# Closing the first two tiles of expert 0 one pair of batches earlier, in an attention and mixture-of-experts kernel

## The chip, the core and the metric

The kernel runs on one core of a Trainium2 chip. The core has TensorE (PE) for matrix products, VectorE (DVE), ScalarE (ACT) and GpSimd (POOL) for the rest, and SyncE (SP), which here only issues transfers; ACT and POOL issue some too. Each engine works through its own instructions in order and waits for others by semaphores. What is measured is the device time of one execution in microseconds (us); lower is better.

## The reference

A sliding-window attention (8 batches, 8 heads, 576 tokens, head size 64, window 64) gives a matrix x of 4608 tokens by 512. A mixture of 8 experts then takes each token to the one expert with the largest logit, with no token dropped:

```python
scores = scale * np.matmul(q, k.transpose(0, 1, 3, 2))
mask = (rel >= 0) & (rel < window)            # window = 64
...
x = attn_out.transpose(0, 2, 1, 3).reshape(B * S, H * D)
logits = x @ w_gate
expert_idx = np.argmax(logits, axis=1)
gate_w = probs[np.arange(N), expert_idx]
...
for e in range(E):
    h = np.maximum(x_sorted[lo:hi] @ w1[e], 0.0)   # 512 -> 1024
    y_sorted[lo:hi] = h @ w2[e]                    # 1024 -> 512
...
return (gate_w[:, None] * y)
```

All of it is in float32.

## The kernel before

**Attention.** Batches are taken in four pairs (`bg` 0 to 3, 1152 tokens each, held as 9 groups of 128), and each pair in four pairs of heads. A pair of batches and a pair of heads is a unit; there are 16 units of 3 steps, so N = 48 steps. `step(s)` (line 896) writes out by hand, in one order for all engines, pieces of several steps at once: scores of step s+1 (`scored`, line 550, into PSUM banks 0 and 1), mask and maximum (`masked`, DVE line 585), exponentials (ACT line 595), the product with v of step s-1 (`weighted`, line 618, bank 6), the logits of step s-3 (line 655, bank 7), transposes of the probabilities of step s (`flipped`, lines 603 and 605), the division (`divided`, DVE lines 628 to 632), transposes of q and k for step s+3 (lines 539 and 531) and of x for step s-2 (`x_turned`, line 643). Then come the operations that were put down in `todo` for this step.

**Routing.** When a pair's logits are there, `after` (line 833) spreads over the next steps: `choose` (line 677) in five parts, which finds the expert, the gate and each token's rank within its expert, and adds to `count`; `place` (line 744), two DVE operations (line 746) for each group of 128 tokens, which write one-hot rows of token numbers; `weigh` (line 751), which multiplies the 512 values of 128 tokens by their gates; and `store` (line 759), which writes the scaled x to `x_dram`. The last pair's routing is written out after the loop, between the products of the first tile.

**Tiles.** The experts work on tiles of 256 tokens, gathered from `x_dram` by indirect transfers that POOL issues. The list of tokens in each slot, `perm_i`, is itself made by products of one-hot tables (`slot_table`, line 779; PE line 807, 72 products). Tiles 0 and 1, both of expert 0, don't wait for that list: `first_tiles` (line 857) picks their 512 tokens out of the first three pairs with a smaller table of its own, `hi_e`, and 54 products (line 869) into `perm_e`. So that no later token gets a slot in them, `choose` sets the count of expert 0 to at least 512 after the third pair (line 730). `gather_first` (line 277) gathers the rows into `xg`.

One tile is a chain of generators: `hidden` (line 314), seven products (PE line 322) in a Strassen form, whose sums of w1 are made ahead on POOL; `turn` (line 299), eight transposes of the next tile's rows (PE line 303) copied by ACT (line 304) to `xq`; and `output` (line 367), seven products (PE line 362), with `sums_x` (DVE line 311), four sums of the turned rows, and four DVE sums of the hidden values (line 139). `sums_w2` (line 152) makes the four sums of w2 on POOL (line 139), into the memory of q and k turned. After the attention loop (line 932 on) the pieces of tile 0 and of the last pair's routing alternate by hand: `next(tile0)` issues one product of the tile, `next(routing)` one part of `choose`, `weigh_some` three scalings on ACT and their store on SP. Tile 0's rows are gathered in step 45 by `first_tiles`, tile 1's after the loop. Two lines set the order around the change:

```python
for n, s in enumerate((N - 6, N - 3)):    # halves of w2 of expert 0, on SP
for _ in range(8):                        # line 984: next(tile0); next(table, None)
```

Behind tile 1 the loop over the experts follows (line 1000 on), with its bodies under conditions on the counts, and at the end `finish` and a last `scatter` (line 288), two indirect transfers to the output, which are declared as having no dependence on the other scatters.

Of the kernel before, what the change touches and what calls it, by code (L numbers as in the profile page):

```python
# [36 lines left out]
def kernel(  # L37
# [10 lines left out]
    nc = tc.nc  # L48
# [164 lines left out]
    hi_e = rt.tile([P, NJE, NE * C], BF16, name="hi_e")  # L213
# [63 lines left out]
    def gather_first(tokens):  # L277

        for c in range(C):
            G.memset(xg[c], 0.0)  # L280

            G.indirect_dma_start(
                out=xg[c], out_offset=None, in_=x_dram[0 : NT - BG * S, :],
                in_offset=bass.IndirectOffsetOnAxis(ap=tokens[:, c : c + 1], axis=0),
                bounds_check=NT - BG * S - 1, oob_is_err=False,
            )
# [12 lines left out]
    def turn():  # L299

        for c in range(C):
            for g in range(NG):
                nc.tensor.transpose(out=tps[c][:, g, :], in_=xg[c][:, g * P : (g + 1) * P], identity=ident[:])  # L303
            nc.scalar.copy(out=xq[:, :, c], in_=tps[c].rearrange("p (a g) s -> p a g s", a=2))
        yield

    def sums_x():
# [132 lines left out]
    with tc.manual_schedule(), ExitStack() as held, ExitStack() as brief:  # L440
# [236 lines left out]
        def choose(bg):  # L677
# [50 lines left out]
            if bg == last - 1:  # L728

                V.tensor_scalar_max(count[:, 0:1], count[:, 0:1], float(NE * TB))  # L730
# [48 lines left out]
        def slot_table(hi):  # L779
# [29 lines left out]
            for j in range(NJE):  # L809
                fill(j)  # L810
            for n in range(NST):
                for m in range(ST):
                    place(NJE + n * ST + m)
                yield
# [18 lines left out]
        def after(s, routing, bg):  # L833
# [3 lines left out]
            if bg < last - 1:  # L837
# [8 lines left out]
                return  # L846

            for n in (0, 0, 1, 2, 2):
                do(n, part)
            for m in range(NTB):  # L850
                do(3 + m // 3, partial(place, bg * NTB + m))
                do((2, 2, 3, 3, 4, 4, 4, 5, 5)[m], partial(weigh, bg, m, nc.scalar if m in (2, 6) else G))
                if m % ST == ST - 1:
                    do(3 + m // ST, partial(store, bg, m // ST, G))
            do(6, first_tiles)

        def first_tiles():

            V.scalar_tensor_tensor(
                out=key[:], in0=rkhi[:, 0:NJE], scalar=1.0, in1=oh_all[:, 0, 0:NJE], op0=ALU.add, op1=ALU.mult  # L860
            )
            V.tensor_tensor(
                out=hi_e[:], in0=_inner(key[:], NE * C), in1=_ins(hi_id[:, C + 1 : C + 1 + NE * C], 1, NJE),
                op=ALU.is_equal,
            )
            slots = banks[next(tr_ring)](0, NE * C)
            for j in range(NJE):
                for i in range(2):
                    nc.tensor.matmul(
                        slots, lhsT=lo[:, i, j], rhs=hi_e[:, j], start=(i + j == 0), stop=(i + j == NJE)  # L870
                    )
            V.tensor_scalar(out=perm_e[:], in0=slots, scalar1=-1.0, scalar2=float(NT), op0=ALU.mult, op1=ALU.add)
            gather_first(perm_e[:, 0:C])
# [55 lines left out]
        for n, s in enumerate((N - 6, N - 3)):  # L929
            fs = slice(n * HF, (n + 1) * HF)  # L930
            todo.setdefault(s, []).append(partial(nc.sync.dma_start, out=w2s[0][:, fs], in_=w2v[0][:, fs]))
        for s in range(-3, N):
            step(s)
        assert not todo
        sums_w2(0)
# [4 lines left out]
        tile0 = chain(hidden(0), turn(), output(0))  # L940
        px = weighted(N - 1, pTs.pop(N - 1))
        form_all(turn())
# [3 lines left out]
        sums_x()  # L946
        gather_first(perm_e[:, C : 2 * C])
        by_tok = [by_tokens(last, c) for c in range(NST)]
        next(by_tok[0])
        next(tile0)  # L950
        logit(N - 2)
        x_turned(N - 1)
        next(by_tok[0], None)
# [23 lines left out]
        next(tile0)  # L977
        next(routing, None)
        weigh_some(2)
# [4 lines left out]
        for _ in range(8):  # L984
            next(tile0)
            next(table, None)
        assert next(tile0, None) is None
# [55 lines left out]


# [26 lines left out]
```

## Time and profile before

| | |
|---|---|
| timed runs, median of 3 | 765.55 us (763.72 to 765.71) |
| the profiled execution, own time | 764.28 us |
| its span, first to last instruction | 762.4 us |
| busy: PE / DVE / ACT / POOL | 94% / 52% / 35% / 47% |
| granted PE clock, mean | 0.986 |
| step 39 of the attention starts | 169.65 us |
| last attention product (line 618) ends | 213.9 us |
| turn of tile 1's rows (line 303) starts | 230.05 us |
| products of the full slot table end | about 247.3 us |
| last scatter starts | 758.05 us |

Busy time is the time in which an engine has an instruction under way; a busy PE isn't PE at its peak, since products are pipelined. The clock is the share of full speed that PE was granted. In a timeline a row is a group of like instructions: start, duration, engine, line, operation, what is written and read, and in brackets how long the engine stood idle before it and which instruction ended that. Line numbers are those of the kernel before.

### The profile page before, as it was taken

What the parts mean: (1) busy time and instruction counts of PE and PEld (TensorE: products, weight loads), DVE (VectorE), ACT (ScalarE), POOL (GpSimd) and SP (SyncE); (2) the same over time, 40 slices, a digit from 0 to 9 for tenths busy, and PEclk for the clock granted to TensorE, in tenths of its full rate; (3) what the DMA queues carried; (4) which work ended last, traced back from release to release, by engine and by line L of the source; (5) the groups of instructions that cost most, each with busy time, mean ns of one, the idle gap of its engine ahead of it and who ended that gap; (6) DMA issues with size and microseconds to landing.
All of it is one profiled execution on the core that took longest, in us unless ns stands there. A gap on an engine that the chain in (4) does not pass through costs nothing. (4 is left out here: it accounts for less than half of the span.)

```text
span 762.4 us, 18401 instructions
## 1 busy us (share of the span) xinstructions
PE 720.1 (94%) x7018; PEld 650.5 (85%) x7018; DVE 395.0 (52%) x1355; ACT 268.4 (35%) x676; POOL 357.1 (47%) x366
## 2 busy tenths in 40 slices
PE   4999999999899999999999999999999999999995
PEld 3888888887688988998999899899988899988994
DVE  2677997988758544523542353352434452424432
ACT  4888888887543201211121122011220121211220
POOL 5215558593860635537531653663266465262111
PEclk8999999999899999999999999999999999999998
DMA  8997889983513712604410360542171171101101
GB/s 162 226 205 173 175 181 255 213 225 113 195 42 126 277 58 67 229 29 138 159 56 30 96 208 30 166 142 70 31 257 45 40 254 56 43 24 42 43 29 54
DMA packets 137620, 94.55 MB, mean 124 GB/s; under 512 B 117072, under 2 KB 117072, under 8 KB 137490
## 3 DMA queue, kind: packets, MB, share of 16 engines
q1 hardware_dynamic: 127858, 62.16, 29.8%
q0 software_dynamic: 9056, 28.58, 11.7%
q10 hardware_dynamic: 576, 2.10, 0.8%
q8 instruction: 78, 1.28, 0.7%
q14 instruction: 52, 0.43, 0.2%
HBM read 73.94 MB, written 20.45 MB: 124 GB/s over the span
## 5 line engine op out<-in xcount | busy, mean ns | idle before, releaser
L322 PE MATMUL bank<-qk_m,s 128*128 128x128 f32 x1216 | 145.4, 275 | 0.0
L322 PEld LDWEIGHTS bank<-qk_m,s 128*128 128x128 f32 x1216 | 140.4, 192 | 0.0
L322 PE MATMUL bank<-qk_m,w 128*128 128x128 f32 x912 | 112.2, 276 | 12.5 <-DVE v_m L358 8.8
L272 POOL DMA_INDIRECT qk_m<-x_dram,at_g x42 | 44.6, 1063 | 167.5 <-PE bank L303 160.2
L322 PEld LDWEIGHTS bank<-qk_m,w 128*128 128x128 f32 x912 | 106.7, 192 | 17.5 <-issue 17.3
L595 ACT ACTIVATE pr<-pr,mx 128x128 f32<-128x128 f32 x288 | 89.7, 390 | 31.8 <-DVE mx L585 31.5
L358 DVE TENSOR_TENSOR v_m<-bank,v_m 128x256 f32<-128x256 f32 x101 | 40.8, 422 | 110.1 <-PE bank L362 54.8
L585 DVE CUSTOM_DVE_ANT_0 pr<-bank,mask 128x128 f32<-128x128 f32 x288 | 64.4, 286 | 27.7 <-PE bank L572 26.1
L329 ACT COPY qk_m<-bank 128x512 f32<-128x512 f32 x19 | 11.2, 587 | 165.7 <-PE bank L322 155.2
L292 POOL DMA_INDIRECT out_dram<-v_m,at_s x42 | 42.4, 1010 | 56.5 <-DVE v_m L358 44.7
L139 POOL TENSOR_TENSOR s<-w 128x1024 f32<-128x1024 f32 x22 | 52.3, 2376 | 19.1 <-DMA qk_m<-x_dram,at_g 14.8
L362 PE MATMUL bank<-qkT_m,v_m 128*128 128x256 f32 x240 | 54.0, 380 | 1.7 <-DVE v_m L139 1.7
L362 PEld LDWEIGHTS bank<-qkT_m,v_m 128*128 128x128 f32 x240 | 45.4, 190 | 8.5 <-DVE v_m L139 2.5
L362 PE MATMUL bank<-qk_m 128*128 128x256 f32 x224 | 52.1, 380 | 0.0
L513 POOL COPY v_m<-v_m 64x520 f32<-64x520 f32 x32 | 19.8, 618 | 67.0 <-DMA v_m<-in_v_dram 59.7
L618 PEld LDWEIGHTS bank<-v_m,pT 128*64 128x64 f32 x1152 | 40.5, 139 | 11.6 <-DVE xs L632 5.8
L618 PE MATMUL bank<-v_m,pT 128*64 128x65 f32 x1152 | 47.2, 229 | 2.6 <-DVE xs L632 2.6
L362 PE MATMUL bank<-s,v_m 128*128 128x256 f32 x216 | 48.1, 379 | 0.0
L362 PEld LDWEIGHTS bank<-qk_m 128*128 128x128 f32 x224 | 41.5, 190 | 5.5 <-ACT v_m L374 0.4
L362 PEld LDWEIGHTS bank<-s,v_m 128*128 128x128 f32 x216 | 41.0, 190 | 5.6
L572 PE MATMUL bank<-qkT_m 64*64 64x128 f32 x1152 | 44.8, 286 | 0.1
L539 PE MATMUL bank<-ident,qk_m 128*128 128x128 f32 x256 | 36.6, 287 | 8.7 <-DMA qk_m<-in_q_dram 8.1
(167 smaller groups left out, 1220.7 us busy)
## 6 DMA issues: line engine op xcount, KB each, us to landing
w<-in_moe_w_dram SPq DMA_DIRECT2D x11, 2048.0 KB, 9.2
qk_m<-in_q_dram SPq DMA_DIRECT2D x72, 128.0 KB, 3.8
qk_m<-in_k_dram SPq DMA_DIRECT2D x72, 128.0 KB, 3.7
v_m<-in_v_dram SPq DMA_DIRECT2D x64, 128.0 KB, 3.7
qk_m<-in_moe_w_dram SPq DMA_DIRECT2D x3, 2048.0 KB, 16.1
x_dram<-xs POOLq DMA_DIRECT2D x6, 512.0 KB, 4.8
x_dram<-xs POOLq DMA_DIRECT2D x3, 768.0 KB, 5.3
w<-in_moe_w_dram ACTq DMA_DIRECT2D x4, 512.0 KB, 5.0
```

Source lines behind the costliest of these rows:

```text
L139: op()
L272: G.indirect_dma_start(out=xg[c], out_offset=None, in_=x_dram[:, :], in_offset=bass.IndirectOffsetOnAxis(ap=at_g[:, c : c + 1], axis=0),)
L292: put = G.indirect_dma_start(out=out[:, :], out_offset=bass.IndirectOffsetOnAxis(ap=at_s[:, c : c + 1], axis=0), in_=ys[c], in_offset=None ...
L322: nc.tensor.matmul(acc[:, f, :], lhsT=a[:, g, f * P : (f + 1) * P], rhs=b[:, g, :], start=(first and f == 0 and g == 0), stop=(g == HG - 1 ...
L358: plus = lambda out, a, b: V.tensor_tensor(out=out, in0=a, in1=b, op=ALU.add)
L362: nc.tensor.matmul(acc, lhsT=a[:, f, :], rhs=b[:, f, :], start=(start and f == 0), stop=(stop and f == HF - 1), skip_group_check=True,)
L513: nc.gpsimd.tensor_copy(out=vb[0:D, i].rearrange("p j h d -> p (j h d)"), in_=va[D:P, i].rearrange("p j h d -> p (j h d)"),)
L539: nc.tensor.transpose(out=tr.rearrange("d a b -> d (a b)").rearrange("d (p j) -> d j p", j=NV)[:, j, :], in_=t[:, c, j].rearrange("p h d - ...
L572: nc.tensor.matmul(out_, lhsT=qT[rows, t, a * WINDOW : (a + 1) * WINDOW], rhs=rhs, start=True, stop=True, skip_group_check=True,)
L585: V.tensor_tensor_reduce(out=prs[h][:, m, :], in0=scs[h][:, m, :], in1=mask[:, m0 + m, :], scale=-scale, scalar=-2 * MASKED, op0=ALU.add, ...
L595: nc.scalar.activation(out=y, in_=y, func=AF.Exp, scale=-1.0, bias=mx[:, h, m : m + 1])
L618: nc.tensor.matmul(px[a * D : (a + 1) * D, h, m, :], lhsT=pTs[h][:, m, a * D : (a + 1) * D], rhs=vt[:, h, :], start=True, stop=True, skip_ ...
```

## The change

Tile 0 is filled from the first two pairs alone (`count` of expert 0 is set to at least 256 after the second pair, and to at least 512 after the third), and tile 1 from the first three, so each gets its own small table: `first_tile(n)` replaces `first_tiles` and is a generator with two halves, the table on DVE and then the products, the list and the gather. Tile 0's halves go to steps N-10 and N-9; its turn and `sums_x` to step N-2, with banks 0 and 1 for the turned rows, and its first hidden product to step N-1. `sums_w2(0)` moves from behind the loop to step N-1, and the halves of w2 are loaded one step earlier. The halves of tile 1's table stand in the tail around the second hidden product.

For the third pair, the five parts of `choose` go to five steps, not three; its scalings are all on POOL, its stores on SP, and its `place` operations two to three steps later. In the tail the last three scalings on ACT move behind the turn of tile 1, and in `slot_table` the 54 products of the early groups move behind the second trio of `place`. At the very end POOL writes one column of each output buffer `ys`, which it can do only when the last scatter has read them.

```diff
@@ -210,7 +210,7 @@
     early, at, rk = (rt.tile([P, NJ], F32, name=n) for n in ("early", "at", "rk"))
     NJE = NJ - NTB
     key = rt.tile([P, NJE], BF16, name="key")
-    hi_e = rt.tile([P, NJE, NE * C], BF16, name="hi_e")
+    hi_e = rt.tile([P, NJE, C], BF16, name="hi_e")
     at_b = rt.tile([P, NJ], BF16, name="at_b")
 
     def starts():
@@ -274,15 +274,15 @@
                 in_offset=bass.IndirectOffsetOnAxis(ap=at_g[:, c : c + 1], axis=0),
             )
 
-    def gather_first(tokens):
+    def gather_first(tokens, rows):
 
         for c in range(C):
             G.memset(xg[c], 0.0)
 
             G.indirect_dma_start(
-                out=xg[c], out_offset=None, in_=x_dram[0 : NT - BG * S, :],
+                out=xg[c], out_offset=None, in_=x_dram[0:rows, :],
                 in_offset=bass.IndirectOffsetOnAxis(ap=tokens[:, c : c + 1], axis=0),
-                bounds_check=NT - BG * S - 1, oob_is_err=False,
+                bounds_check=rows - 1, oob_is_err=False,
             )
 
     def scatter(tokens):
@@ -296,7 +296,7 @@
             tc.declare_no_dep(put.ins, group="puts", reason="every token has one slot, so no row is written twice")
             tc.add_to_no_dep_group("puts", put.ins)
 
-    def turn():
+    def turn(tps=tps):
 
         for c in range(C):
             for g in range(NG):
@@ -304,7 +304,7 @@
             nc.scalar.copy(out=xq[:, :, c], in_=tps[c].rearrange("p (a g) s -> p a g s", a=2))
         yield
 
-    def sums_x():
+    def sums_x(tps=tps):
 
         b12, b22, b21 = tps[1][:, 0:HG], tps[1][:, HG:], tps[0][:, HG:]
         for n, (a, b) in enumerate(((b12, xq[:, 0, 0]), (b22, xs[:, 0]), (b22, xq[:, 0, 1]), (xs[:, 1], b21))):
@@ -725,9 +725,9 @@
             rank = new("r_rank", E, NTB)
             V.tensor_tensor(out=rank[:], in0=inc[:], in1=_inner(count[:], NTB), op=ALU.add)
             V.tensor_tensor(out=count[:], in0=count[:], in1=inc[:, :, NTB - 1], op=ALU.add)
-            if bg == last - 1:
-
-                V.tensor_scalar_max(count[:, 0:1], count[:, 0:1], float(NE * TB))
+            if last - NE <= bg < last:
+
+                V.tensor_scalar_max(count[:, 0:1], count[:, 0:1], float((bg - last + NE + 1) * TB))
             V.tensor_tensor(out=rank[:], in0=rank[:], in1=ranks[:, 1], op=ALU.subtract)
             V.tensor_tensor(out=rank[:], in0=rank[:], in1=ranks[:, 0], op=ALU.add)
             yield
@@ -806,11 +806,12 @@
                 for i in range(2):
                     nc.tensor.matmul(slots, lhsT=lo[:, i, j], rhs=hi[:, j], start=(i + j == 0), stop=(i + j == NJ))
 
-            for j in range(NJE):
-                fill(j)
             for n in range(NST):
                 for m in range(ST):
                     place(NJE + n * ST + m)
+                if n == 1:
+                    for j in range(NJE):
+                        fill(j)
                 yield
             for j in range(NJE, NJ):
                 fill(j)
@@ -844,33 +845,36 @@
                     if m % ST == ST - 1:
                         do(5 + m * 2 // 3, partial(store, bg, m // ST, G))
                 return
-
-            for n in (0, 0, 1, 2, 2):
+            for n in range(5):
                 do(n, part)
+
             for m in range(NTB):
-                do(3 + m // 3, partial(place, bg * NTB + m))
-                do((2, 2, 3, 3, 4, 4, 4, 5, 5)[m], partial(weigh, bg, m, nc.scalar if m in (2, 6) else G))
+                do((5, 5, 6, 6, 7, 7, 8, 8, 8)[m], partial(place, bg * NTB + m))
+                do((3, 3, 4, 4, 5, 5, 6, 6, 7)[m], partial(weigh, bg, m, G))
                 if m % ST == ST - 1:
-                    do(3 + m // ST, partial(store, bg, m // ST, G))
-            do(6, first_tiles)
-
-        def first_tiles():
-
+                    do(5 + m // ST, partial(store, bg, m // ST, nc.sync))
+
+        def first_tile(n):
+
+            nj = (last - NE + n + 1) * NTB
             V.scalar_tensor_tensor(
-                out=key[:], in0=rkhi[:, 0:NJE], scalar=1.0, in1=oh_all[:, 0, 0:NJE], op0=ALU.add, op1=ALU.mult
+                out=key[:, 0:nj], in0=rkhi[:, 0:nj], scalar=1.0, in1=oh_all[:, 0, 0:nj], op0=ALU.add, op1=ALU.mult
             )
             V.tensor_tensor(
-                out=hi_e[:], in0=_inner(key[:], NE * C), in1=_ins(hi_id[:, C + 1 : C + 1 + NE * C], 1, NJE),
-                op=ALU.is_equal,
-            )
-            slots = banks[next(tr_ring)](0, NE * C)
-            for j in range(NJE):
+                out=hi_e[:, 0:nj], in0=_inner(key[:, 0:nj], C),
+                in1=_ins(hi_id[:, (n + 1) * C + 1 : (n + 2) * C + 1], 1, nj), op=ALU.is_equal,
+            )
+            yield
+            slots = banks[next(tr_ring)](0, C)
+            for j in range(nj):
                 for i in range(2):
                     nc.tensor.matmul(
-                        slots, lhsT=lo[:, i, j], rhs=hi_e[:, j], start=(i + j == 0), stop=(i + j == NJE)
+                        slots, lhsT=lo[:, i, j], rhs=hi_e[:, j], start=(i + j == 0), stop=(i + j == nj)
                     )
-            V.tensor_scalar(out=perm_e[:], in0=slots, scalar1=-1.0, scalar2=float(NT), op0=ALU.mult, op1=ALU.add)
-            gather_first(perm_e[:, 0:C])
+            to = perm_e[:, n * C : (n + 1) * C]
+            V.tensor_scalar(out=to, in0=slots, scalar1=-1.0, scalar2=float(NT), op0=ALU.mult, op1=ALU.add)
+            gather_first(to, nj * P)
+            yield
 
         N = NU * NST
         load_qk(0)
@@ -926,30 +930,36 @@
                     after(s + 1, choose(bg), bg)
 
 
-        for n, s in enumerate((N - 6, N - 3)):
+        for n, s in enumerate((N - 7, N - 4)):
             fs = slice(n * HF, (n + 1) * HF)
             todo.setdefault(s, []).append(partial(nc.sync.dma_start, out=w2s[0][:, fs], in_=w2v[0][:, fs]))
+
+        tile0 = chain(hidden(0), turn(), output(0))
+        first = first_tile(0)
+        todo.setdefault(N - 10, []).append(partial(next, first))
+        todo.setdefault(N - 9, []).append(partial(next, first))
+        free = [banks[i](0, NG, P) for i in (0, 1)]
+        todo.setdefault(N - 2, []).extend((lambda: form_all(turn(free)), partial(sums_x, free)))
+        todo.setdefault(N - 1, []).extend((partial(next, tile0), partial(sums_w2, 0)))
         for s in range(-3, N):
             step(s)
         assert not todo
-        sums_w2(0)
 
 
 
         tr_ring = cycle((4, 5))
-        tile0 = chain(hidden(0), turn(), output(0))
         px = weighted(N - 1, pTs.pop(N - 1))
-        form_all(turn())
         logit(N - 3)
         divided(N - 1, px)
         x_turned(N - 2)
-        sums_x()
-        gather_first(perm_e[:, C : 2 * C])
+        second = first_tile(1)
+        next(second)
+        next(tile0)
         by_tok = [by_tokens(last, c) for c in range(NST)]
         next(by_tok[0])
-        next(tile0)
         logit(N - 2)
         x_turned(N - 1)
+        next(second)
         next(by_tok[0], None)
         next(by_tok[1])
         next(tile0)
@@ -974,16 +984,16 @@
         next(tile0)
         starts()
         weigh_some(1)
-        next(tile0)
         next(routing, None)
-        weigh_some(2)
         next(tile0)
         brief.close()
         hi = held.enter_context(tc.tile_pool(name="hot", bufs=1)).tile([P, NJ, NS], BF16, name="hi")
         table = slot_table(hi)
-        for _ in range(8):
+        for n in range(8):
             next(tile0)
             next(table, None)
+            if n == 0:
+                weigh_some(2)
         assert next(tile0, None) is None
         gather(perm_i[:, 3 * C : 4 * C])
         finish()
@@ -1041,6 +1051,9 @@
         finish()
         scatter(perm_i[:, bass.ds(end * C, C)])
 
+        for c in range(C):
+            G.memset(ys[c][:, 0:1], 0.0)
+
 
 # ---- launch: one core; inputs and outputs as the reference has them ----
 _INS = ['q', 'k', 'v', 'moe_w_gate', 'moe_w1', 'moe_w2']
```

## The prediction

> **What bounds the kernel now.** I read the page's rows of busy time first. TensorE (PE) is busy 94% of the span, and in the tile loop it hardly waits. So a change can win only where PE stands still or runs at a low clock, and the slices show where that is: between 180 and 215 us, at the end of the attention steps, which is where the change is made. The timeline of PE there:
>
> ```profile
> 184.66 1.04 PE L539 MATMUL bank<-ident,qk_m 128*128 128x128 f32 x8
> 187.11 0.55 PE L643 MATMUL bank<-ident,xs 128*128 128x128 f32 x3 [1.41 <-DVE pT L605]
> ...
> 198.94 0.49 PE L643 MATMUL bank<-ident,xs 128*128 128x128 f32 x3
> 202.13 1.56 PE L869 MATMUL bank<-hi_e,lo 128*128 128x4 bf16 x54 [2.70 <-DVE hi_e L862]
> 203.63 1.55 PE L572 MATMUL bank<-qkT_m 64*64 64x128 f32 x24
> 205.11 1.62 PE L618 MATMUL bank<-v_m,pT 128*64 128x65 f32 x24
> ...
> 239.57 1.91 PE L807 MATMUL bank<-hi,lo 128*128 128x62 bf16 x54 [1.29 <-DVE qk_m L311]
> ```
>
> [...] Steps are counted from the first L572 of each: step 39 starts at 169.65, 42 at 181.89, 44 at 191.66, 45 at 195.07, 46 at 203.63. In step 42 PE waits 1.41 for VectorE (DVE), which does two parts of the routing in one step. In step 45 it waits 2.70 for hi_e. After that wait the same 24 L572 take 1.55 where they take 0.89 in other steps. The reason is the clock, in the table by stretches (us, busy time of each engine, PEclk, DMA share, GB/s):
>
> ```profile
> 199.50:202.00 2.50, 0.00 (x0) 0.00 (x0) 2.40 (x14) 2.38 (x8) 2.20 (x3) 1.00 0.13 38
> 202.00:203.70 1.70, 1.57 (x58) 1.55 (x60) 0.08 (x1) 0.22 (x1) 1.14 (x3) 0.63 0.79 255
> 203.70:209.70 6.00, 5.73 (x65) 4.51 (x65) 2.89 (x17) 2.59 (x8) 3.14 (x4) 0.54 0.33 98
> ```
>
> **What the change takes away**, each from such a row:
> - The four-column table in step 45: the wait of 2.70 and 1.50 of products: 4.20. Its key and hi_e are now made a step (or a product) ahead of the products that need them.
> - The low clock after it: L572 1.55 for 0.89, L618 1.62 for 0.97, L655 0.65 for 0.42, L603 1.54 for 0.88, L643 0.84 for 0.49: 2.55.
> - The 1.41 of step 42, since the routing parts go one to a step: DVE then has 2.63 of its own (six L585 at 0.21, L605 0.47, L628/L629/L632 0.89) and one part of 1.3 to 1.4, 4.0 beside PE's 4.07.
> - Smaller waits: 0.24 at 178.3; in step 44/45, 0.54 in a stretched L572 and 0.48 before L618, both because three groups of tokens are placed in one step; 0.27 and 0.88 before the last two L618, which now have the turn (1.0) and a product (1.9) of tile 0 ahead of them: 2.41.
> - The 1.29 at 239.57: the 54 early table products now stand behind one more output product, by when hi is ready.
>
> Sum: 11.86.
>
> **What it adds.**
> - Products of tables: 36 + 54 of two columns for 54 of four. The 54 took 1.50 start to start, 0.028 each (two columns for four saves nothing that I count): 1.0 in step 39, 1.5 in the tail, both on PE's path: 2.5.
> - The place operations (L746) slide from steps 42 to 44 into 44 to 47, and sums_x of tile 0 (1.63) comes into step 46. From the start of step 44 to the last but one division DVE has 0.95 (until the first scores are there) + 3 × 2.63 + 1.63 + 1.36 + 12 places at 0.22 = 14.5; PE reaches the product that needs it after 3.42 + 3.2 + 4.1 + 4.2 = 14.9 (steps 44 and 45 as measured between waits, 46 with the turn, 47 with the first product). With undisturbed places that nearly fits; DVE's own wait for the copies of the turned tile (about 1.1) then leaves 0.75 of PE wait. But the places now lie beside GpSimd (POOL) work: nine scalings at 1.56 in a row (about 183.8 to 197.8) and then sums_w2 (about 198.7 to 208.2). Beside a scaling the rows show
>
> ```profile
> 191.82 0.30 DVE L746 TENSOR_SCALAR lo<-lane,low,tok_a 128x128 bf16<-128x128 bf16 x1
> 192.04 0.81 DVE L746 TENSOR_SCALAR lo<-lane,low,tok_b 128x128 bf16<-128x128 bf16 x1
> 192.66 0.30 DVE L746 TENSOR_SCALAR lo<-lane,low,tok_a 128x128 bf16<-128x128 bf16 x1
> 192.88 0.74 DVE L746 TENSOR_SCALAR lo<-lane,low,tok_b 128x128 bf16<-128x128 bf16 x1
> ```
>
>   and six of them in 2.4, 0.40 each. Twelve at 0.40 add 2.2: I take 3.0 of PE wait, in pieces under 1.3.
> - The chain of ScalarE (ACT) behind the last gates. From 226.11 to 234.51 ACT is busy without a break (nine scalings, three relus, two copies, the copy y1), and the third output product, at 234.56, needs y1 out of its bank. Tile 0 has one hidden product fewer left between the gates and this point, so PE comes 1.87 earlier, and the nine scalings still stand ahead of y1: moving the last three behind the turn's copies leaves them ahead of y1. So PE waits 1.87 there. The 1.41 and 1.44 gaps of this trace did not lower the clock (1.00 after 302.6), so neither should this.
> - The two one-column memsets wait for the last scatter. It starts at 758.05 and lands 2.8 later (the median of this row), 760.85; the chain's last drain ends at 761.2 and traffic is over by 761.0. So the wait is nearly there already: no gain, since the drain comes after it; at most 0.7 (two memsets under the 0.54 of a 512-column one, partly hidden). I take 0.2, near the lower end.
>
> **At nothing**, with what covers it. Two scalings leave ACT (0.73 each; it idles 2 to 3 in steps 42 to 45). The stores of pair 2 go from POOL's queue to SP's, behind two w2 loads whose second half (1 MB, 6.0 to land) comes first; the scatter of tile 0's tokens no longer waits for them, and tile 1's gather comes 10 us later. POOL no longer sits out the 8.08 it waited at 190.35 for a scaling on ACT. Tile 0's gather (two memsets 0.54, two issues 1.02) goes to about 178, behind POOL's copies of v, when POOL is nearly idle, 20 us before its turn. Tile 1's gather stands behind sums_w2 (4 × 2.36): the table ends about 4.9 after the last L618, the gather has landed at 11.3, its turn comes at 14.8: 3.5 of cover, and if that is gone PE waits at the turn. The places of the last pair end on DVE 0.8 before PE wants them. The extra maximum is one 0.15 operation and pads nothing: on these inputs expert 0 has 421 tokens after two pairs and 538 after three, over the 256 and 512 asked for, so the tiles stay the same.
>
> **Sum:** 11.86 − 2.5 − 3.0 − 1.87 − 0.2 = 4.3. The profiled execution took 764.28: 760.0. The three timed runs have their median at 765.55, but with the profiled one the mean is 764.8, 0.5 above it; I forecast **760.5**.
>
> [...] First, the clock. [...] Here 2.70 was enough (0.63, then 0.54 for 6 us). [...]
>
> ```profile
> 261.33 2.67 DVE L139 TENSOR_TENSOR v_m<-qk_m 128x512 f32<-128x512 f32 x1 [0.75 <-ACT qk_m L350]
> 264.04 2.72 DVE L139 TENSOR_TENSOR v_m<-v_m,qk_m 128x512 f32<-128x512 f32 x1
> 266.68 2.83 DVE L139 TENSOR_TENSOR v_m<-qk_m 128x512 f32<-128x512 f32 x1
> 269.44 0.68 DVE L139 TENSOR_TENSOR v_m<-qk_m,v_m 128x512 f32<-128x512 f32 x1
> ```
>
> 0.69 became 2.7 for each, a whole POOL operation of 2.36 waited out. [...]
>
> **Rivals.** A change under 0.3% (2.3 us) can't be told from none.
> - *Forecast* (places slowed as beside scalings): 760.5, range 758.9 to 762.5. Chance 0.50.
> - *Places hardly slowed:* PE waits 0.75, not 3.0: 758.2. For it: the median place takes 0.31 and only some of those beside scalings are slow. Against: in the new order nearly all lie beside POOL. Chance 0.22.
> - *The lock on sums_w2:* 2.6 more, and the one piece is then over 2.7, so the clock falls again, 2.55: 765.6, no change. For it: the L139 row. Chance 0.16.
> - *The lock on all places,* the other side: in steps 44 and 45 four pairs wait about 0.8 each (half of 1.56), in step 46 two pairs 2.36 each, together 7.9, with 1.1 for the turn's copies and less 0.4 of slack 8.6, and 2.55 of clock: 11.2 for my 3.0, so 768.7. It decides against the change from about 7.3 of wait on. Against: the worst place of the trace took 0.96. Chance 0.12.
>
> **Range and chances.** 756.8 to 766.0 leaves out the last case and part of the second: it holds about 8 in 10. Faster is nearly all of the first two, 0.70; the same 0.17; slower 0.13.
>
> **What would show it.** The table products of step 39 without a wait ahead of it, and clock 1.00 from there to the tail; the L807 group without its 1.29; a new wait of about 1.9 at the third output product, put down to ACT; L746 after 198 at 0.4 (forecast) or over 2 (lock); the last drain still about 3 us after the last scatter. I am wrong if PE's wait before the last two L618 is over 2.5, or if the turn of tile 1 waits for its gather.

## The result, and the profile after

The changed kernel takes 771.5 us (median of 4, 769.34 to 772.55); the kernel before took 765.63 in the same comparison (763.72 to 766.18). The ratio is 1.0077, with a 95% interval of 1.0049 to 1.0106: slower, where 760.5 and faster was forecast. The profiled execution took 771.0 itself, its span is 769.2 (before: 764.28 and 762.4).

The timeline of PE after the change, for the stretch shown of before:

```profile
175.66 1.04 PE L871 MATMUL bank<-hi_e,lo 128*128 128x2 bf16 x36
...
197.37 1.12 PE L618 MATMUL bank<-v_m,pT 128*64 128x65 f32 x24 [0.48 <-DVE xs L632]
...
207.62 1.75 PE L303 MATMUL bank<-ident,qk_m 128*128 128x128 f32 x8 [4.24 <-DVE mx L585]
209.62 1.62 PE L618 MATMUL bank<-v_m,pT 128*64 128x65 f32 x24 [0.24 <-DVE xs L632]
...
218.88 1.49 PE L871 MATMUL bank<-hi_e,lo 128*128 128x2 bf16 x54
...
237.15 1.99 PE L362 MATMUL bank<-qk_m 128*128 128x256 f32 x8 [1.85 <-ACT v_m L374]
...
242.44 1.74 PE L807 MATMUL bank<-hi,lo 128*128 128x62 bf16 x54
```

Both small tables (L871) come without a wait ahead of them, the 1.41 of step 42 is gone, and so is the 1.29 ahead of L807. What was won there is spent in one piece: at 207.62 PE has waited 4.24 for DVE before it turns tile 0. What it waits for is the attention maxima (L585): they read the scores out of PSUM banks 0 and 1, which the change gives to the turned rows, and in DVE's order they stand behind the places. The table by stretches (length, busy time of PE, PE's weight loads, DVE, ACT, POOL, then PEclk, DMA share, GB/s) shows the clock behind that wait:

```profile
202.00:207.60 5.60, 1.38 (x15) 0.96 (x9) 5.60 (x11) 0.42 (x2) 5.52 (x4) 1.00 0.42 153
207.60:209.40 1.80, 1.75 (x8) 1.13 (x8) 1.73 (x10) 1.80 (x7) 1.80 (x2) 0.64 0.00 0
209.40:216.00 6.60, 6.38 (x86) 5.53 (x87) 5.26 (x20) 2.80 (x7) 0.27 (x1) 0.84 0.01 2
```

In the first row DVE and POOL are busy all or nearly all the time, PE for 1.38 of 5.60. The timeline of DVE in it, and below it that of POOL:

```profile
200.74 1.41 DVE L746 TENSOR_SCALAR lo<-lane,low,tok_a 128x128 bf16<-128x128 bf16 x1
202.07 0.30 DVE L746 TENSOR_SCALAR lo<-lane,low,tok_b 128x128 bf16<-128x128 bf16 x1
202.30 2.35 DVE L746 TENSOR_SCALAR lo<-lane,low,tok_a 128x128 bf16<-128x128 bf16 x1
204.56 2.38 DVE L746 TENSOR_SCALAR lo<-lane,low,tok_b 128x128 bf16<-128x128 bf16 x1
206.86 0.28 DVE L585 CUSTOM_DVE_ANT_0 pr<-bank,mask 128x128 f32<-128x128 f32 x1
```

```profile
199.74 2.36 POOL L139 TENSOR_TENSOR qkT_m<-qk_m 128x1024 f32<-128x1024 f32 x1
202.18 2.42 POOL L139 TENSOR_TENSOR qkT_m<-qk_m,qkT_m 128x1024 f32<-128x1024 f32 x1
204.55 2.34 POOL L139 TENSOR_TENSOR qkT_m<-qk_m 128x1024 f32<-128x1024 f32 x1
206.85 2.36 POOL L139 TENSOR_TENSOR qkT_m<-qkT_m,qk_m 128x1024 f32<-128x1024 f32 x1
```

The place operation that starts at 200.74 ends about when POOL's operation ends, at 202.10; the one at 202.30 ends with POOL's second, at 204.6; the one at 204.56 with its third. Only the one at 202.07 fits between two. Four operations of 0.3 stretch over 6.2. The maxima behind them, beside POOL's fourth, are not held.

The other loss is at the very end of the kernel. The timeline of POOL, before:

```profile
754.84 1.02 POOL L292 DMA_INDIRECT out_dram<-v_m,at_s  x1 [4.48 <-DVE v_m L358]
758.05 1.00 POOL L292 DMA_INDIRECT out_dram<-v_m,at_s  x1 [2.19 <-issue]
```

and after:

```profile
755.79 1.02 POOL L292 DMA_INDIRECT out_dram<-v_m,at_s  x1 [4.86 <-DVE v_m L358]
757.12 1.01 POOL L292 DMA_INDIRECT out_dram<-v_m,at_s  x1 [0.30 <-issue]
759.93 0.13 POOL L1055 MEMSET v_m<- 128x1 f32 x2 [1.81 <-DMA out_dram<-v_m,at_s]
```

Before, POOL paused for 2.19 between the last two scatters, for no reason that the profile names. After the change the pause is gone, and yet the end is later. The view of the kernel's last source line has POOL's drains (operations of that name that come behind the kernel's last instruction; count, shortest, median and longest in ns, then the first and last start). Before:

```profile
L1066 POOLq DRAIN  x3: 46/112/3363, 757.8 to 762.1; - x3
```

and after:

```profile
L1079 POOLq DRAIN  x3: 46/113/8418, 759.9 to 768.9; - x3
```

The first of the three is the long one: 3.36 before, ended at 761.2; 8.42 after, ended at 768.3. No data moves while it lasts after the change. In the table of DMA traffic from 750 to 772, in 40 slices of 0.55, the changed kernel moves nothing after the 18th slice, 759.9:

```profile
GB/s 0 0 30 0 0 0 0 0 30 0 0 0 0 231 134 97 372 8 0 0 0 0 0 0 0 0 0 0 0 0 0 0 0 0 0 0 0 0 0 0
```

So the two spans, 6.8 apart, are made up as follows (us, both profiled executions):

| | before | after | difference |
|---|---|---|---|
| start of step 38 | 166.08 | 168.13 | +2.04 |
| step 38 to the end of the last L618 | 47.91 | 47.47 | −0.44 |
| to the end of the full table's products | 33.27 | 32.64 | −0.63 |
| to the end of the last output product (L362) | 506.12 | 506.10 | −0.02 |
| to the start of the last but one scatter | 1.46 | 1.45 | −0.01 |
| to the end of POOL's long drain | 6.35 | 12.54 | +6.19 |
| to the end of the span | 1.2 | 0.9 | −0.3 |

### The profile page after: what moved, and what is told of

The parts are those of the page before. It is cut to its first block, busy times and chain, and to the rows that moved or that the text cites. A ratio compares the mean times of both kernels' runs of the same rounds, so it can differ in the third digit from the quotient of the medians.

```text
span 769.2 us, 18491 instructions
## 1 busy us (share of the span) xinstructions
PE 721.3 (94%) x7054; PEld 651.7 (85%) x7054; DVE 398.8 (52%) x1359; ACT 266.9 (35%) x674; POOL 356.6 (46%) x364
## 3 DMA queue, kind: packets, MB, share of 16 engines
q0 software_dynamic: 8384, 26.22, 10.4%
## 5 line engine op out<-in xcount | busy, mean ns | idle before, releaser
L585 DVE CUSTOM_DVE_ANT_0 pr<-bank,mask 128x128 f32<-128x128 f32 x288 | 64.3, 287 | 28.0 <-PE bank L572 26.6
L329 ACT COPY qk_m<-bank 128x512 f32<-128x512 f32 x19 | 11.1, 587 | 164.1 <-PE bank L322 162.8
L139 POOL TENSOR_TENSOR s<-w 128x1024 f32<-128x1024 f32 x22 | 52.3, 2377 | 17.5 <-DMA qk_m<-x_dram,at_g 13.2
L362 PE MATMUL bank<-qkT_m,v_m 128*128 128x256 f32 x240 | 54.0, 380 | 1.1 <-DVE v_m L139 1.1
L362 PE MATMUL bank<-qk_m 128*128 128x256 f32 x224 | 52.1, 380 | 1.9 <-ACT v_m L374 1.9
L362 PEld LDWEIGHTS bank<-qkT_m,v_m 128*128 128x128 f32 x240 | 45.4, 190 | 7.9 <-DVE v_m L139 1.9
L618 PEld LDWEIGHTS bank<-v_m,pT 128*64 128x64 f32 x1152 | 41.3, 140 | 10.5 <-DVE xs L632 4.6
L618 PE MATMUL bank<-v_m,pT 128*64 128x65 f32 x1152 | 48.1, 231 | 1.5 <-DVE xs L632 1.4
L362 PE MATMUL bank<-s,v_m 128*128 128x256 f32 x216 | 48.1, 379 | 0.0
L362 PEld LDWEIGHTS bank<-qk_m 128*128 128x128 f32 x224 | 41.5, 190 | 7.4 <-ACT v_m L374 2.3
L362 PEld LDWEIGHTS bank<-s,v_m 128*128 128x128 f32 x216 | 41.0, 190 | 5.6
```

The costliest lines, as they stand in the source:

```text
L139: op()
L362: nc.tensor.matmul(acc, lhsT=a[:, f, :], rhs=b[:, f, :], start=(start and f == 0), stop=(stop and f == HF - 1), skip_group_check=True,)
L585: V.tensor_tensor_reduce(out=prs[h][:, m, :], in0=scs[h][:, m, :], in1=mask[:, m0 + m, :], scale=-scale, scalar=-2 * MASKED, op0=ALU.add, ...
L618: nc.tensor.matmul(px[a * D : (a + 1) * D, h, m, :], lhsT=pTs[h][:, m, a * D : (a + 1) * D], rhs=vt[:, h, :], start=True, stop=True, skip_ ...
```

## The experiments

Four theories were tried. A: the last memsets carry the loss. B: places beside the sums of w2 wait out POOL's operations, and the clock falls behind that wait. R: the stores of pair 2, moved from POOL's queue to SP's, lower the number of transfers that POOL issues (106 DMA instructions on POOL before, 100 after, counted in the records of the traces), and with it the pause becomes a long drain. C: `hi_e` has half its size, so what lies behind it in SBUF has moved, and the early transfers are slower. R came up only after the first four runs. Ratios are to the kernel before on the same chip. "The change without memsets" is e1. In the expectations of f1, f2 and f4 "the last pair" is pair 2, the last but one.

**e1_no_end**, **e2_end_only**, **e3_end_on_dve**, **e4_end_no_wait**: the memsets taken from the change, and put alone on the kernel before.

```diff
 e1, from the change:
-        for c in range(C):
-            G.memset(ys[c][:, 0:1], 0.0)
 e2, from before:
+        for c in range(C):
+            G.memset(ys[c][:, 0:1], 0.0)
 e3: V.memset in e2's place; e4: G.memset(xs[:, c, 0, 0:1], 0.0), which waits for no scatter
```

> The changed kernel without the two last memsets. Theory A (the end carries the loss: POOL's last drain lasts 8.4 us behind memsets, 3.4 us behind a scatter): the time from the last product to the end of the span falls from 14.9 to about 9.0 us, and the kernel comes to about 765.6, the same as before within 1.5. Theory B (the lock on the places and the clock behind it carry the loss): it stays at 770 to 771.5, since nothing in the attention steps is changed.

> The kernel before with only the two last POOL memsets added. Theory A: 5 to 6.5 us slower than before, about 771, the drain near 8.4 us. Theory B: under 1 us slower, since only the wait for the last scatter and 0.13 us of memset are added.

> The kernel before with the two last memsets on DVE, so that the wait for the last scatter is there but POOL's last instruction is a scatter. If the wait itself is dear: about 6 us slower. If it is POOL's drain behind a memset: within 0.5 us of before, the drain at about 3.4 us.

> The kernel before with two last POOL memsets of one column each in the sums of x, which no scatter reads, so POOL's last instruction is a memset without a wait for the scatter. If it is the drain behind a memset: as slow as with the wait, 4 to 6.5 us slower than before, the drain over 8 us. If the wait is what costs: within 0.5 us of before.

| | median (lowest to highest) | ratio, 95% interval |
|---|---|---|
| e1 | 771.61 (768.24 to 774.01) | 1.0061, 1.0039 to 1.0082 |
| e2 | 766.84 | 1.0007, 0.9994 to 1.0021 |
| e3 | 766.06 | 0.9995, 0.9985 to 1.0004 |
| e4 | 766.28 | 0.9998, 0.9983 to 1.0014 |

Theory A falls as the main cause: without the memsets most of the loss stays, and on the kernel before they cost at most 1.6. In e1's profile the last two scatters follow each other by 1.33, as in the change, and its long drain takes 10.0.

**f2_before_stores_sp** and **f1_stores_back**: the six stores of pair 2 alone, in both directions.

```diff
 f2, from before:
-                    do(3 + m // ST, partial(store, bg, m // ST, G))
+                    do(3 + m // ST, partial(store, bg, m // ST, nc.sync))
 f1, from e1:
-                    do(5 + m // ST, partial(store, bg, m // ST, nc.sync))
+                    do(5 + m // ST, partial(store, bg, m // ST, G))
```

> The kernel before with only the six stores of the last pair on SP's queue. Theory R: 100 transfers by POOL, a gap of 0.3 between the last two scatters, 12 to 15 us from the last product to the end of the span where before has 9.1, and the median 3 to 5 above before, 769.5 to 771.5. Rival B: no difference at the end, and the time within 1 of before, if anything below it, since the stores wait for nothing on POOL any more.

> The change without its last memsets, and with the six stores of the last pair back on POOL's queue instead of SP's. Theory R (the count of transfers that POOL issues, 100 instead of 106, moves a housekeeping pause out of the tile loop and into the final drain): the 2.2 us pause stands between the last two scatters again, the last output product is followed by about 9 us and not 12.9 to 14.9, and the median falls from 771.6 by 3 to 5, to 766.5 to 768.5, no longer different from before by more than 2. Rival B (all of the loss is the lock and the clock in steps 45 and 46): the end still takes about 9 or 13 as chance has it, and the median stays at 771 to 772.

f2: 770.07 (768.76 to 771.73), ratio 1.0064 (1.0051 to 1.0077). One edit, on the kernel before, costs 4.4, and its profile shows the same end as the change, in POOL's timeline:

```profile
755.63 1.02 POOL L292 DMA_INDIRECT out_dram<-v_m,at_s  x1 [4.66 <-DVE v_m L358]
756.95 0.99 POOL L292 DMA_INDIRECT out_dram<-v_m,at_s  x1 [0.30 <-issue]
```

and in the view of the last line:

```profile
L1066 POOLq DRAIN  x3: 46/112/9980, 756.2 to 766.8; - x3
```

The drain starts at 756.2 and lasts 9.98, to 766.2. That moving these stores lengthens the end is shown by this edit; why is taken up below. f1 undoes it: the pause of 2.19 is back and the drain is 3.37 long, but the median is 769.6, ratio 1.0057 (1.0039 to 1.0074), higher than R's 766.5 to 768.5. The profile says where: with six issues more on POOL the sums of w2 start 36.4 behind the start of step 38, for 31.6 in the change, the places of step 47 now meet them, PE waits 4.59 before the last L618, and from the start of step 38 to the table's end it takes 82.6 where e1 takes 80.1. So the stores were moved off POOL's queue for a reason, too; what was not seen is the price at the other end.

**g1_last_stores_pool**: the same count by other transfers. The stores of the last pair, which come when POOL has nothing else to do, go from SP to POOL; those of pair 2 stay on SP.

```diff
 from e1, in weigh_some:
-            store(last, c, nc.sync)
+            store(last, c, G)
```

> The change without its last memsets; the six stores of pair 2 stay on SP's queue as the change has them, and the six stores of the last pair go to POOL's queue instead, where POOL has nothing else to do. POOL issues 106 transfers again, but other ones. Theory R in the form 'the count decides': the pause of 2.2 stands between the last two scatters, the end takes about 9 instead of 12.9, steps 38 to the tables' end take 80 as in the change, and the median is 3.5 to 4.5 below that of the change without memsets, 767 to 768. Rival R2, 'it is the stores of pair 2 themselves (where in the program POOL issues them) that decide': the end stays at 12.9 and the median at 771 to 772.

767.15 (765.7 to 772.58), ratio 1.0021 (1.0004 to 1.0038), as expected, with the pause back, and 6.38 from the start of the last but one scatter to the end of the long drain, where e1 has 10.59. So it is not the stores of pair 2 as such; six other transfers of the same sizes, issued at 230 to 238 where the kernel before has its six at 190 to 203, do the same.

**h1_change_106** (this edit on the change itself, memsets kept) and **h4_sp_and_end** (f2 with the two memsets, on the kernel before) ask what the memsets cost with either drain.

```diff
 h1, from the change, in weigh_some:
-            store(last, c, nc.sync)
+            store(last, c, G)
 h4, from f2, behind the last scatter:
+        for c in range(C):
+            G.memset(ys[c][:, 0:1], 0.0)
```

> The whole change, its last memsets too; only the six stores of the last pair go to POOL's queue instead of SP's, so that POOL issues 106 transfers and not 100. If the count is what costs, the end falls from 14.9 to 9 to 9.7 and the median from 771.5 to 766 to 767; if the memsets carry 2 of the 14.9 by themselves, the end is 11 and the median 767.5 to 768.5.

> The kernel before with the stores of pair 2 on SP and the two last memsets, and nothing else of the change. f2, without the memsets, took 4.4 more than before. If the memsets hold back the long drain, as the end of 14.9 beside 12.9 in the profiles says: 2 more than f2, 772 and an end of 14 to 15. If they cost as little here as with the short drain (0.5): 770 to 771 and an end of 12.9 to 13.4.

h1: 769.03 (766.88 to 771.77), ratio 1.0025 (1.0008 to 1.0043). h4: 772.9 (770.99 to 775.47), ratio 1.0089 (1.006 to 1.0118). In h1 the end is as R says, 6.91, though the median is 2 to 3 above the number given. Its profile has the rest in two places that no theory names: step 38 starts at 169.75 (168.13 in the change), and from the table's end to the last output product it takes 507.7 (506.1). This last stretch takes 507.1 to 508.3 in f3, f4, g1, g2, g3, h1 and h3, and 505.5 to 506.3 in all the others; the cause is not known. In h4 the end is 12.52, and the median is near the 772 of its first case. With it the table of the end is complete; every kernel falls into one of these rows:

| POOL's transfers | kernels | pause before the last scatter | start of the last but one scatter to the end of the long drain |
|---|---|---|---|
| 100 | e1, f2, f3, f5 | none | 10.57 to 10.59 |
| 100, with memsets on POOL that wait | the change, h4 | none | 12.54, 12.52 |
| 106 | before, e3, e4, f1, f4, g1, g2, g3 | 2.19 | 6.34 to 6.38 |
| 106, with memsets on POOL that wait | e2, h1 | 2.19 | 6.90, 6.91 |
| 108, 112 | h3, h2 | none | 6.98, 7.06 |

The memsets cost 0.55 with the short drain and 1.95 with the long one: by the traces the long drain starts only behind them, at 759.9 in the change, while without them it starts at 756.2 (f2), beside the scatters. The two prices add up to the whole: 6.35 + 4.22 + 1.95 = 12.52.

**h2_before_112** and **h3_thin_108** ask whether the number itself matters (h3 is told below).

```diff
 h2, from before, in weigh_some:
-            store(last, c, nc.sync)
+            store(last, c, G)
```

> The kernel before with the six stores of the last pair on POOL's queue as well: POOL issues 112 transfers. If the pause of 2.2 comes at a fixed number of transfers (the 106th), it falls among the gathers of the tile loop, where POOL has time, the last two scatters follow each other by 1.3, and the end is 2 shorter than before or as long: 763.5 to 766. If it is the place in the program and not the number, nothing changes: 766. If a larger count only starts the next round of the housekeeping, the long drain comes back: 769 to 771.

765.3 (763.25 to 769.13), ratio 0.9991 (0.9971 to 1.0012). No pause before the last scatter, and yet the end is no shorter than before; the drain of 6.48 takes the pause's place. Only half of the expectation held. The gap ahead of the 104th transfer is 1.14 where it is 0.30 at that place in before, and 1.95 for 0.63 in h3; the profile puts both down to ACT, so that they are the pause, at about the number of before's 106th, is a guess. Nor is the number told apart from what the transfers carry: with 100, 106, 108 and 112 of them, the profiles count 8384, 9056, 9120 and 9728 packets in POOL's queue. What POOL does in the pause and in the drain the traces do not show; that it is housekeeping, as theory R in f1 and the last case of h2 have it, is the author's guess.

**f3_no_sums_w2** takes the other partner of the lock away. It leaves out the sums of w2 of expert 0, so the tiles of expert 0 are computed with sums that were never made.

```diff
 from e1:
-        todo.setdefault(N - 1, []).extend((partial(next, tile0), partial(sums_w2, 0)))
+        todo.setdefault(N - 1, []).append(partial(next, tile0))
```

> The change without its last memsets, and without the sums of w2 for expert 0 (they are left out, so the tiles of expert 0 are computed with old sums). Theory B (four places of steps 45 and 46 each sit out a POOL operation of 2.4): without POOL operations after 199.8 the places take about 0.3 each, the turn no longer waits 4.24 in front of its products, the clock stays at 1.00 there, and the stretch from step 38 to the last L618 shrinks from 47.5 to 41 to 43; the end is as long as in the change (12.9 to 14.9); in all 5 to 6 below 771.6, about 766. Theory R alone: the stretch stays above 46 and the median at 770 to 772.

766.43 (764.34 to 767.39), ratio 1.0008 (0.9997 to 1.0019) where e1 has 1.0061: some 4 less, with the long drain unchanged. Its timeline of DVE

```profile
199.80 0.30 DVE L746 TENSOR_SCALAR lo<-lane,low,tok_a 128x128 bf16<-128x128 bf16 x1
200.02 0.31 DVE L746 TENSOR_SCALAR lo<-lane,low,tok_b 128x128 bf16<-128x128 bf16 x1
200.25 0.31 DVE L746 TENSOR_SCALAR lo<-lane,low,tok_a 128x128 bf16<-128x128 bf16 x1
200.47 0.31 DVE L746 TENSOR_SCALAR lo<-lane,low,tok_b 128x128 bf16<-128x128 bf16 x1
```

has the same four place operations at 0.3, its PE timeline has the turn without a wait, and the table by stretches has the clock at full:

```profile
199.90:206.00 6.10, 5.84 (x86) 4.83 (x86) 4.77 (x24) 4.18 (x12) 0.53 (x1) 1.00 0.57 214
```

Step 38 to the last L618 takes 42.2, for 47.5. B is shown, as the second cause.

**f4_both**, **g2_thin_sums**, **g3_thin_y1** and **h3_thin_108** try to keep what the change wins. f4 has the stores of pair 2 on POOL, no places in steps 45 and 46, and the last three scalings behind the copy y1; g2 is g1 with the sums of w2 in pieces of a quarter; g3 is g2 with the scalings behind y1; h3 is g3 with two early loads on POOL.

```diff
 f4, from f1:
-                do((5, 5, 6, 6, 7, 7, 8, 8, 8)[m], partial(place, bg * NTB + m))
+                do((5, 5, 5, 8, 8, 8, 8, 8, 8)[m], partial(place, bg * NTB + m))
 f4 and g3, in the loop of the tail:
-            if n == 0:
+            if n == 1:
                 weigh_some(2)
 g2, from g1, in place of sums_w2(0):
+            for f in range(HF):
+                form(right_sums(G, s2s[0][:, :, f : f + 1], *(w[:, f : f + 1] for w in w2q(0))))
 h3, from g3, lines 881 and 882:
-        nc.sync.dma_start(...
+        G.dma_start(...
```

> The change without its last memsets, with the stores of the last pair on POOL, no place in steps 45 and 46 (three in 44, six in 47), and the first of the last three scalings behind the copy y1 in the tail. Theories R and B together: 3 to 5 less at the end, 4 to 6 less in steps 45 and 46 and up to 1.9 less at the third output product, so 759 to 763, below before by 3 to 7. If only R holds, 766 to 768; if only B, 763 to 766.

> g1 with the sums of w2 of expert 0 in sixteen POOL operations of 256 columns instead of four of 1024; the same work, each operation about 0.6 to 0.65 instead of 2.36. Theory B, 'a place waits out the POOL operation that runs': each place of steps 45 and 46 takes at most about 0.9, PE's wait of 4.24 in front of the turn's products falls to 0 to 1.5, the clock stays at 1.00, steps 38 to the last L618 take 42 to 44 (47.5 in the change), and the median is 4 to 5 below g1, 762.5 to 764. Rival B2, 'POOL's traffic as such slows the places, whatever the size of its operations': places still take 2.3 in pairs, and the time is that of g1 within 1.

> g2 with the last three scalings of the last pair behind the copy y1 in ACT's order, one product later. The wait of 1.85 at the third output product goes; if nothing else is late behind it, 1.5 to 1.9 below g2, 761 to 762.5, and below before by 3 to 4.5. If the later scalings only move the wait to another product (the stores of the last tokens or the copies after), the time is that of g2.

> The version g3 with the load of the gate's weights and that of the row of zeros, both at the start, on POOL's queue: POOL issues 108 transfers. By a fixed number the pause moves two transfers ahead, off the end: 762 to 763. If not, 764.2 as g3.

| | median (lowest to highest) | ratio, 95% interval | step 38 to last L618 | to the table's end |
|---|---|---|---|---|
| f4 | 765.2 (763.69 to 767.8) | 0.9995, 0.9982 to 1.0007 | 44.1 | 35.5 |
| g1 | 767.15 | 1.0021, 1.0004 to 1.0038 | 47.4 | 32.7 |
| g2 | 766.04 (763.07 to 769.76) | 1.0004, 0.9986 to 1.0023 | 44.8 | 32.7 |
| g3 | 764.2 (763.13 to 768.01) | 0.998, 0.9965 to 0.9995 | 44.9 | 31.9 |
| h3 | 762.66 (761.4 to 768.08) | 0.9955, 0.9934 to 0.9976 | 44.9 | 31.9 |

f4 misses its 759 to 763: the first two of the twelve place operations of step 47 still lay beside the sums (1.30 and 2.86), PE waited 2.11 for the last division instead, and the clock fell behind that. In g2 the sums are made in pieces, and a place operation waits for one piece:

```profile
202.30 0.77 DVE L746 TENSOR_SCALAR lo<-lane,low,tok_b 128x128 bf16<-128x128 bf16 x1
202.99 0.76 DVE L746 TENSOR_SCALAR lo<-lane,low,tok_a 128x128 bf16<-128x128 bf16 x1
```

```profile
202.29 0.73 POOL L139 TENSOR_TENSOR qkT_m<-qk_m 128x256 f32<-128x256 f32 x1
202.98 0.72 POOL L139 TENSOR_TENSOR qkT_m<-qkT_m,qk_m 128x256 f32<-128x256 f32 x1
```

The place operations of step 45 take 0.57 to 0.77, the wait of 4.24 is 0.67, and the clock stays at full. The stage gains 2.6, less than expected, since small delays remain (0.48, 0.67, 0.70 and 1.13 of PE), and the median 1.1, where it was to come to 762.5 to 764. In g3 the wait of 1.85 at the third output product is gone, and nothing is late right behind it: 0.8 of that stage in the profile, 1.8 in the median, which still misses its 761 to 762.5. h3 is faster than both kernels, by 3.4 to 3.7 than before, and has the 762 to 763 expected of it; but that its two extra transfers did it is not shown, for its end, from the last product to the end of the span, is 9.25, as long as g3's 9.06. What h3's profile has ahead of g3's is an earlier start of step 38 (167.8 for 169.5).

**f5_old_size** is for theory C.

```diff
 from e1:
-    hi_e = rt.tile([P, NJE, C], BF16, name="hi_e")
+    hi_e = rt.tile([P, NJE, NE * C], BF16, name="hi_e")
```

> The change without its last memsets, with hi_e at its old size of four columns per group (only the first two are written and read), so that everything placed behind it in SBUF lies where it lay before. Theory C (the shifted addresses slow the transfers of the first 60 us and with them all that follows): step 38 starts 2 to 4 earlier than in the change without memsets (172.7) and in most runs, and the median falls to 767 to 769. If the early part differs from execution to execution whatever the layout, the median stays within 1 of 771.6.

769.83 (767.72 to 771.34), ratio 1.0051 (1.0031 to 1.0071), against e1's 1.0039 to 1.0082. It lies between the two expectations, and the intervals overlap; the profiled execution starts step 38 at 166.5. C is not shown. The start of step 38 lies anywhere from 165.3 (h4) to 172.7 (e1) in the seventeen other traces, and at 166.1 and 169.9 in the kernel before and h2, which share every instruction up to there. So of the +2.04 in the table nothing can be laid to the change from these traces, and what of the 5.9 of the medians is not in the end and the stages (6.19 − 1.07 − 0.3 = 4.8; 1.1 remain) stays open, within an interval of 3.8 to 8.1.

## Why the prediction was wrong

Against the 760.0 worked out for the profiled execution it took 771.0. The steps of the sum, one by one:

- *The table of step 45 and its wait, 4.20; the 1.41 of step 42; the 1.29 ahead of L807:* right, all three are gone.
- *Products of two tables, 2.5:* right, 1.04 + 1.49.
- *The third output product waits for ACT's chain, 1.87:* right, 1.85; g3 shows the cause, since moving the three scalings behind y1 removes it. That this wait wouldn't lower the clock held in the change (1.00), though not in every kernel (below).
- *The small waits, 2.41:* 0.48, before L618 in step 44, is still there, and 0.24 before a later one; both are counted in the next step. A new one of 0.47, before L705, was not foreseen.
- *The places beside POOL, 3.0, and no low clock:* the rows of places beside scalings, from which the 3.0 was taken, were the wrong ones. PE's waits there are 0.48 + 4.24 + 0.24 = 4.96, 1.96 more, and the low clock that follows costs 1.51 (L303 1.75 for 1.04, L618 1.62 for 0.97, L655 0.57 for 0.42). Place operations beside scalings were as cheap as taken, 0.31 to 0.60. Those beside the sums of w2 went as the L139 row, where DVE's sums beside POOL's sums of weights took 2.67 to 2.83: a place waited for the end of the POOL operation that it met (2.35 and 2.38, beside 2.42 and 2.34). One row could not stand for both partners. The rival "the lock on sums_w2" had the mechanism, f3 and g2 show it, and "the lock on all places" is refuted. Its size was off even so: the 2.6 more is the author's estimate, which no run shows; in its place PE waited 1.96 more, as two POOL operations and a part of a third were sat out (6.2 for four place operations that take 1.0 in f3), and the clock cost 1.51, not 2.55. Together 3.5, about the stage's shortfall: forecast −4.5, measured −1.07.
- *The stores of pair 2 "go from POOL's queue to SP's" at nothing:* **this is the step that turned the sign.** It was judged by the queues it is moved between and by who waits for the stores; that was right, and f1 shows it even helped. But the transfers that POOL issues decide how the kernel ends: with six fewer the end is 4.22 longer in the profiles, and f2 is 4.4 slower by its median. No rival had it; the statement that a drain of about 3 must follow the last scatter was given as a sign, and it failed (8.42).
- *The last memsets, 0.2 (0 to 0.7):* 0.55 with the drain they were judged by, inside the bounds; 1.95 with the long one.
- *The gather of tile 1 in time, the maximum, the gather of tile 0:* right, none shows up as a wait.

The end was underestimated by 5.7 (6.19 less the 0.2 counted and the 0.3 behind it), the stage by 3.4, and the start of step 38 was 2.0 late, which is not laid to the change: 11.1, beside the 11.0 to be explained. Less the end's 4.22 and 1.95 the change would stand at about 765.3. g1, which is the change with neither, takes 767.15 where before takes 766.27, with 2.2 more in its tile loop that nothing explains. Either way no gain is left: the lock had eaten most of it by itself.

## What to carry to other kernels

When a change moves transfers to or from GpSimd's queue, look at the end of the kernel in both traces, at the pause between the last transfers and at the length of the last drain, though the moved step lies hundreds of microseconds earlier; six transfers put back on that queue, at a place where it is idle, can cost less than the drain (g1 767.15, e1 771.61). A short VectorE operation beside GpSimd is to be priced by the trace of the very operation it will lie beside, and cutting GpSimd's operation into pieces bounded the wait here (a place took at most 0.77 in step 45 of g2, beside pieces of 0.72 to 0.73, and 2.38 beside the whole operations of 2.34 to 2.42). And look at the clock behind the longest wait that is left in the new order: here it cost 1.51 more.

## What the runs showed of the hardware

- The end described above: with 100 transfers issued by POOL its last drain takes 8.4 to 10.0, in the change with no DMA traffic in it; with 106 it takes 3.3 to 3.4 behind a pause of 2.19 (0.9 where the memsets wait ahead of it), and with 108 and 112 it takes 6.4 to 6.5 without a pause. From the last but one scatter to the end of the drain, the lengths in a row of the table agree to 0.08. Why is open.
- The low clock around the change comes in pieces of two lengths. Cut at its edges it reads 0.50, and it lasts 3.4 (208.15 to 211.50 in the change) or 6.8 (202.45 to 209.25 before); the shares between 0.50 and 1.00 above are means over stretches that hold a part of it. It lasted 6.8 behind the 2.70 of before and 3.4 behind the 4.24 of the change: the length of the wait doesn't give the price.
- The same wait can lower the clock or not. PE's 1.85 ahead of the third output product left it at 1.00 in the change and in e1; in f3 it was followed by 0.50 from 232.35 to 235.70, and L362 took 2.52 for 1.99. In f4 2.11 was enough, with a delay: the wait ended at 216.31, the clock fell at 218.95.
- A VectorE operation with one bf16 input and one bf16 output, 0.3 alone, was held to the end of a GpSimd operation on f32 operands that it met (2.35 and 2.38, beside 2.42 and 2.34), while the six attention maxima (L585) beside the next of these operations kept their 0.28 each.
